# Convolution steps in half-array tiles without swaps, output sums per segment and 128 tokens, and a new written-out order

## The chip, the cores and the metric

The kernel runs on one core of one Trainium2 chip. The metric is device time in microseconds. An execution has five engines with queues of their own: TensorE (PE, with its weight loads PEld), VectorE (DVE), ScalarE (ACT), GpSimd (POOL, nearly unused here) and SP, which issues the transfers. Each works through its own instructions in order and waits on semaphores for the others.

## The reference

Input x has 2048 tokens of 512 features. Two branches are computed from it and mixed with a gate per token.

```
g = sigmoid(sum(x * gate_w))                      # one number per token
# branch a: 32 heads of 16, four segments of 512 tokens
for s in 0..3:
    p  = softmax(q_s k_s^T * 0.25 + causal mask);  dot = p v_s
    mem = phi(q_s) M / (phi(q_s) z + 1e-6)         # M, z: sums over earlier segments
    o_s = sigmoid(beta) * mem + (1 - sigmoid(beta)) * dot
    M += phi(k_s)^T v_s;  z += sum phi(k_s)        # phi(t) = t + 1 if t > 0 else exp(t)
a = concat(o) @ wo
# branch b: a long convolution along the tokens, a kernel of 2048 taps per feature
K[d, l] = Re sum_n C[d,n] exp(dt_d A[d,n] l) dt_d B[d,n]
b = causal_conv(x, K) + x * Dskip                  # the reference takes FFTs of length 4096
out = g * a + (1 - g) * b
```

## The kernel before, in words

**How work gets its order.** build_graph records some 1800 operations with their tiles. A written-out list, ORDER, gives for each operation its place, the engine where there is a choice (evictions from PSUM may go to ScalarE or VectorE) and its buffer; replay and emit put the instructions on the engines in that order and add the semaphores. So nothing is decided at run time: each engine's sequence is that of the list. Matrix multiplies all go through one helper, L687; evictions through L226 (ScalarE) and L227 (VectorE), scaled ones through L229 and L230; transfers through L222 on SP.

**Attention.** For each of four segments and four groups of eight heads (16 pairs), project computes q and k, scores makes five score tiles, so 80 in all. A score tile fills PSUM banks 0 to 3 with multiplies on row tiles of the array (16 or 32 rows, four at a time), is turned into weights by one exponential of 2048 columns (L1069, ScalarE), is masked (L1081, VectorE, or extra multiplies on TensorE for the first eight pairs), and is multiplied with v (pv, 17 columns each). nrm (L1041 to L1044) normalises, mem (L1117 to L1121) adds the memory part, and ophase transposes the result into oT (the operation named oT). All other PSUM users share banks 4 to 7 and, where free, the lower ones.

**Convolution.** ssm_prep, ssm_powers (L795 to L805) and ssm_cb prepare the parameters; x_level1 applies a first level of a 4096-point transform to x over the tokens and stores it in a scratch tensor; tables (L1164, L1167, L1171) builds powers for four groups of 128 features, and lag turns them into kernel taps with multiplies on column tiles of 32 (four at a time). tail then runs, for each half of the 512 features, 16 steps. One step: load two constants (CT of 192 KB, CD of 320 KB) and a piece of the scratch; X, two multiplies of 256 columns, whose real and imaginary parts lie in the two halves of the partitions; an eviction; two transfers of 64 KB that put the halves in swapped places beside it; K, ten multiplies from the taps; an eviction; Y, the product on VectorE (L1273, 1024 columns); V, four multiplies back; an eviction; and a store into V2.

**Output sums.** When tail has a half, it takes its 256 columns for 16 blocks of 128 tokens (every 16th token), two blocks to a PSUM bank: per block four multiplies of attention result with wo (256 columns), two of x with a diagonal matrix (the skip term, 128 columns), two of G2 with V2 (256 columns). Two evictions per bank scale by 1 - g (the branch a was prepared with e^z = g / (1 - g), so one factor serves both), and a store of 256 KB writes four blocks. gate_rows brings the gates into that layout once, with a small multiply. A block holds tokens of all four segments, so no sum can end before the last segment's attention.

**What sets the order there.** In the list all 32 blocks of output sums stand behind the last score and behind the last steps of tail, whose last V steps come between them and the last attention products. Tail's second half starts when the tables' buffers are free, since it lies in their place.

Of the kernel before, what the change touches and what calls it, by code (L numbers as in the profile page):

```python
# [366 lines left out]
9/0 10/1 391/1 15/0 29/0 0/0 23/0/0 24v 30/1 193/0 13/4 14/2 21/0 12/3 11/5 27/1/1 25/2/2 189/0 54/0 31/8 32/0 33/6  # L367
38/2 39/3 57/3 34 190 35 7/0 37/11 20/0 1226/1 28a 36 17/0 45/8 40/4 41 55/4 44/5 26v 46/7 42 173/7 43 48/0 50/9 18/0
51/10 1232/5/0 47 59/1 4/0 56a/0 58v 1244/7/1 1/0 61/4 1242/6 49/12 60 71/0 205/0 62v/0 73/3 178/2 52/0 72 53 85/1
196/3 16/0 74a/3 1234/0 1235a 250/1/0/0 83/0 67/6 1243a 200/4/2/2 65/2 84 191 1233a 208/2 98v/1 181/3 1245a 201a 377/0  # L370
95/1 63 197/0 97/5 86v/9 99 3/0 66 1246 96 192/0 174/0 64 203/5/0 209a 251a 202 107/2 77/1 214/0/0/0 75 76 206/3 1236
108/0 109 252 204a 219/0/3 220 378/2 119/2 79/1 122v/2 110v/4 175/0 198/0 78 379 123 121/4 120 176/0 87 100 588/0 221
253/1/1 240/0/0 241 131/1 177 994v/0 254a 215 179/0 111 133/2 88 998v/0 112 997v 134v/5 1002 1003/0 1247/0 199/1 132
216 210/2 242 145/4 212/1 135 207a 1000/1 146v/6 91/3 1004 228/0/1 229 996v 995v 143/2 89/1 1009/0 144 999 8/0 158v/8
230 147 157/5 213a 255/0/1/1 223/0/2 256 155/2 2/0 799/0 124 1008 1248/3/1 224 90 211a 222/1 1249a 159 1001 1260/2/0
589/3 257 136 225 1250/0 160 1006/1 1010 156 590 1005 1012/0 167v/7 1251a 1252 1014 1258/3 1011 236/0/3 1007 1259a 237
103/0 226 227 231 232/3 1261a 337/0/2 235/3 1013 238 233 168 101/2 800/2 1015/1 1020 234/0 262/0/2 263 239 338a 1262
169 1229/1/1 243 244 801 1016 1263/0/0 102 264 113/1 1230a 1021/0 245/0 217 1227/2 1264a 266/0/1 267 1022 268 1018/1
1265/1 148 1024/0 1023 383/0/1/1 115/7 114 1228a 258 271/0/0 246 127/2 384a 1266a 272 293/2/2/2 273 296/0/0 265/1 1267
279/0/2 280 1231 297a 218/0/0 259 269 270 274 1025 1017 125/2 281 986/0 283/0/3 284 592/0 1032 247 591 1026 1033/0 126  # L380
137/1 1239/3/1 294a 1019 1034 260/0 1237/2 334/0/0/0 285 295 275/1 1035 1240a 307/0/1 308 1268/1 1030/1 278/3 276
1238a 1255/2/0 282 1027/0 335a 277/1 309 1253/1 1289/0 286 287 339/0/0/0 303/0/3 1028 288/1 1254a 1241 1029 340 341
380 304 443/1/1 1036/0 1031 248/0 1037 305 444a 138/4 336 320/0/0 321 289 1256a 1284/1/1 22/0 802 1257 249v/0 1043/2/0
1044 1045 322 290 447/0 139 1046 298/0/1/1 1286/3 1047v 312/0/2 313 194 1285a 182 149/2 150/5 398/2 1287a 195 1038/1
1039 1040 1041 299 301 300 399v 1056v/0 314 1290/3/0 306/0 324/0/3 325 1054v/0 1052v 1291a 1288 1061/1 1053v 1042a
116a/0 310 319/2 1060 1058/0 1055v 311 326 315 1292/3 385 1293a 1048/0 1294 323 1276/1/1 1057 1062 1059 1070/1 316/2
342 1066 1063 346/0/1 347 386/3/0 1277a 317 1069 80v/1 1274/1 318/0 291/0 348 1071 350/0/2 292a 151 351 387a 1300/0/0
1302/3 1067/0 1275a 1078 1079/1 104v/3 1068 1278 327 328 396/1 1080 352 68v/4 81 355/0/0 356 1082/0 1301a 397a 1081
329/3 1073/1 1083 330 1303a 357 349/0 1072 353 1281/1/1 1064/0 331 354 392/3 393a 1282a 1304 1050 1049 1074 1090 69
363/0/3 1091/1 140v/8 1065 364 1075 302/2 358 343 1271/3/0 1092 344 365 359/4 1076/0 1279/1 70 1272a 105 360 141 1280a  # L390
367/0/1 368 369 1051 117 1283 361/1 1085/1 106 1307/2/1 1269/3 1084 1077 1093 1094/0 405/0/2 1086 1270a 1087 406 381
6/0 92a/2 1088/1 407 1095 1089 362/3 1305/1 366 370 1273 1295/0/0 409/0/0 161/1 410 1308a 1306a 411 394/2 490/1/2/2
422/0/3 423 395a 408/2 371 1296a 1297/0 412 413 93 372/1 1309 373 491a 261 440/1/0/0 424 1298a 1310/0 1299 82 94 374
388/0 389 162/0 345 118 1323/1 441a 128v/9 180 163 1390/0 492 426/0/2 427 152v/5 382/0 170v/7 171 442 153 1096/0/1
1097 1098 1099 1101/3 1312/2 332/1 390/1 428 1100a 1102 164a/6 165 333a 414/0/0 415 416 1103 1104 1114v/0 1113v/0 1118
472/0/1 473 417 1119/1 421/0 1325/1 425 448/1/1/1 1110a 1116/0 1105a 1313/3/2 1111a 1120 1112a 474 172 1311/1 429 430
1106 1109 129 130 166 1107 455/0/0 456 1115 1124 1314a 418/5 1128/1 419 1117 420/0 142 1121 431/2 1108 1316 449 450
493/3/0 1324/0 400/2/0/0 457 401 1326/1/0 459/0/3 1327a 460 1125/0 432 1127 433 451 1129 1126 1137/1 1130 1122/0 1136
1317/1/0 1123 461 375/0 1318a 1138 464/0/2 494a 402 465 1315 1338/1 1337/1 466 1139 154 1364/2 1319/1 1328 1329 5/0
541/1/2 458/3 1320/2/0 542a 1321a 476/0/0 462 477 376a 478 1330/1/0 471/2 463 475 1336/0 467 1131/1 1331a 1339/0/2 479  # L400
1340a 520/0/3 480 1140/0 521 403 1141 522 1363/0 1132 1148 1343/1/1 404/0/1 1134/0 1149/1 1344a 452 468/0 1133 481/3
469 1332/0 1342 1341 1322/0 482 495/1 470/1 483 434/1/2/1 512/0/1 1333/1/1 1135 453 435 1334a 1150 1350/1 1351/1 513
514 651/0/0/1 436 1345/1 437 538/1/1/0 1146/0 1346/3/0 1151 1152/1 652a 1347a 524/0/2 498/2/0/0 438/0 1349/1 539a
1352/3/1 439a/0 1362/0 1335 499 803 1353a 1356/1/1 1142 1153 1355 445/0 1354 605/0/0 1365/3/0 1357a 525 519/1 523
1366a 1348 1145 1143/1 1369/3/0 500 1368 597/2/1 526 1144 1367 1370a 606a 598a 1147 1358/0 1389/1 527 528 183/6 529/4
1154/3/0 497/1 446 501 530 1159/0 184/0 1160 1359/2/0 1360a 484/2/1/0 1376/0 546/7/1/1 185/0 1377/1 543/0 540 1371/1
1372/2/1 496 653 547 485 1375/1 486 1416/2 549 487 548 1161 1162 1373a 1388/0 1155 1156 1157 531/0 503/0/2 1374 1163a
187 1378/2/2 1172a/0 1168v/0 504 1169v 1382/1/0 1391/0/1 1170v 1158a 1361 1379a 1174/1 1171v 1177/0 1173 1176 1175
1395/3/1 1429/1 1381 1380 1178 505 1179 1183/1 1182 1428/0 1392a 507/0/0 508 1185 1186/0 1383a 1393 545/0 502/2 1184
1394 1187 609/0 1384/0 550 1442/0 1415/1 1396a 1385/1/0 509 610a 1195/0 553/0/3 1386a 554 506/3 510 1180/1 1194 551  # L410
532/0/5/1 511 515 1414/1 555 1397/1 1398/2/1 1196 516/0 533 517 987/1 518 1399a 1181 557/0/2 599/1 558 534 1417/3/0
1418a 1387 1197 559 1198/0 535 1421/2/0 1427/0 1165 1189/1 1419 1420 1434/3/1 1199 1455/2 1441/1 1188 1430/1/1 1206
1422a 570/0/0 1207/0 571 1431a 594/0/2/2 1167 1433 1432 488/2 1190 1400 1423/0 572 595a 489a 556/1 1208 562/0/1 563
1424/0/0 544 1192/1 1435a 564 654/2/0 655a 1425a 1191 1436/1 1447/3/0 1440/1 574/0/3 1448a 1437/2/1 1193 1210/0 1201/1
603/0 188 1454/0 1443/3/0 1438a 575 604a 1200 560 561 565 1453/0 566/3 1444a 1468/1 536/2 576 1467/1 567 1445 596
1460/0/1 1446 568/1 1456/3/2 616/0/2 1202 1209 1426 537a 1494/0 1457a 569/1 573 577 578 607/2 814/3/1 617 608a 1461a
815a 1204/1 637/0/1 1459 1458 1439 600 1480/0 1449/1 1450/2/0 638 1466/1 1211 1203 1473/3/0 659/0/1/1 1462/0 1474a
1451a 625/0/0 1205 1463/3/1 1217/2/1 1218 1464v 626 1219 1493/1 1469/3/0 1470a 1220 813 620/0/3 1479/0 579/2 618 639
1486/3/1 627 1481/2 602 660 1452 661 619/0 580 1221v 581 621 1212/2 1213 1487v 1471 1472 633/0/2 1403/1 1506/0
1482/1/1 701/3/1/0 988/0 622 623 1483v 704/1/2 624 1507/2 1484 1465 634 454 1475/1 1476/6/0 628 705a 635 593/1 658/1  # L420
1477a 702a 552 629/1 630 1485 1214 1492/1 1215 683/0/3 1499/1/0 632/3 636 1216a 684 703 640 666/0/2 641 1580/0
1495/2/2 631/0 1500a 1582/0 1488/0 1567/1 1489/0/1 1554/2 667 1496v 1512/1/1 670/0/0 1490v 1513a 611/2/0/0 1401/0
1593/3 662 642/4 643 644 582/0/2/1 816/3 668 671 583 1224 584 585 1569/1 1498 1497 731/0/1 1583/0/0 1568/0 612 1478
1402/1 817v 613 749/1/2/2 1570/3/1 732 1404/2/0 1222 1584v 750v 669/0 614 687/0/2 1571a 1405a 1555/1 1595/2 1556/0
601/0 1501/1 1491 672 615/1/0 663 645/1/0/0 664 646 1581/2 757/1/0/0 647 688 648 758 656/1 673 685 674 675/0/0
1502/2/0 1225 759 751 657 1503v 676 586/3 587a 1166 689 1505/1 752/1/1 753a 1164 805/2/0/1 806a 677 695/3/5/1 696 697
# [982 lines left out]
```

## Time and profile before

| what | value |
|---|---|
| three runs | 309.24, 316.8 and 314.4 us; median 314.4 |
| profiled execution, first to last instruction (its span) | 311.0 us; its own time is not given apart |
| mean granted TensorE clock in it | 0.944 of full speed |
| busy: TensorE, VectorE, ScalarE | 264.8, 260.2, 262.7 us |
| instructions: TensorE, VectorE, ScalarE | 4397, 642, 320 |
| exponentials of the scores, L1069 | 80, together 151.9 us |
| moved by the transfers | 45.82 MB, mean 147 GB/s |

How to read the rows: a group of instructions is "line engine operation output<-input shape xcount | busy us, mean ns of one | idle time of the engine just before them, and what ended it". Busy time is the union of the intervals, so for matrix multiplies, which overlap, it is far less than count times mean. PSUM is psum, the on-chip memory is sb. In the table of stretches each engine's number is its busy time in that stretch, with the count of instructions; PEclk is the granted TensorE clock there.

### The profile page before, as it was taken

The page shows a single profiled execution, that of the slowest core. Times are in us where ns is not written, and L with a number is a line of the kernel's source. Part 1 is how long each engine was busy: PE and PEld are TensorE (multiplying, and loading weights), DVE is VectorE, ACT ScalarE, POOL GpSimd, SP SyncE. Part 2 cuts the span into 40 slices and gives each one's busy share as a digit, 9 for nine tenths or more (in the row PEclk, how much of TensorE's full clock was granted, in tenths as well). Part 3 has the DMA queues.
Part 4 walks back from the last instruction along what each step waited for, and adds up shares of the span by engine and source line. Part 5 has one row for each costly group of instructions (what it writes and reads, how often), then busy time and mean ns, then how long its engine had stood idle before and what let it go on. Part 6 is the DMA issues. An engine that isn't in the chain of part 4 may idle for free.

```text
span 311.0 us, 10366 instructions
## 1 busy us (share of the span) xinstructions
PE 264.8 (85%) x4397; PEld 185.1 (60%) x4430; DVE 260.2 (84%) x642; ACT 262.7 (84%) x320; POOL 3.1 (1%) x9
## 2 busy tenths in 40 slices
PE   2678788788779789998999898999999988799991
PEld 1433355454435547676766574676677666579991
DVE  1999899999998889998999868888999898862152
ACT  2999999999999979987999898999999999861150
POOL 2000000000000000000001000000000000000000
PEclk9995689999968779999999999999999999979997
DMA  6878522431232545465555657637555667511143
GB/s 145 280 176 160 142 87 70 124 118 52 83 110 77 160 121 155 147 197 157 158 173 192 199 159 229 196 95 228 156 197 186 200 200 217 168 52 48 38 137 102
DMA packets 54926, 45.82 MB, mean 147 GB/s; under 512 B 22624, under 2 KB 50272, under 8 KB 54880
## 3 DMA queue, kind: packets, MB, share of 16 engines
q1 hardware_dynamic: 54880, 45.16, 49.8%
q8 instruction: 35, 0.57, 0.8%
q14 instruction: 11, 0.09, 0.1%
HBM read 26.92 MB, written 6.29 MB: 107 GB/s over the span
## 4 chain that ended last, share of the span: by engine, by line
ACT 42%; PE 41%; issue 7%; DVE 4%; DMA 3%; SPq 1%; another core or an unknown queue 0%; DVEq 0%; ACTq 0%
PE psum L687 40%; ACT sb L1069 23%; ACT sb L226 13%; ACT sb L795 2%; DMA sb<-sb 1%; DVE sb L227 1%; DMA sb<-c_DNM 1%; DMA sb<-c_ident 1%; SPq L222 1%; ACT sb L803 1%; ACT sb L1000 1%; DVE sb L1273 1%; ACT sb L949 1%; DVE sb L1121 0%; ACT L888 0%
## 5 line engine op out<-in xcount | busy, mean ns | idle before, releaser
L687 PE MATMUL psum<-sb 128*128 128x17 bf16 (+12 forms) x4309 | 257.5, 225 | 32.5 <-ACT sb L1069 14.4
L687 PEld LDWEIGHTS psum<-sb 128*128 128x128 bf16 (+3 forms) x4342 | 178.2, 97 | 109.7 <-issue 29.7
L1069 ACT ACTIVATE sb<-psum 128x2048 bf16<-128x2048 f32 x80 | 151.9, 1899 | 6.7 <-PE psum L687 6.4
L226 ACT ACTIVATE sb<-psum 128x512 bf16<-128x512 f32 (+2 forms) x155 | 88.1, 625 | 8.6 <-PE psum L687 8.1
L227 DVE CAST sb<-psum 128x512 bf16<-128x512 f32 (+1 forms) x47 | 31.3, 676 | 4.8 <-PE psum L687 4.8
L1164 DVE TENSOR_TENSOR sb<-sb 128x512 bf16<-128x512 bf16 (+3 forms) x52 | 33.5, 654 | 0.0
L1167 DVE TENSOR_TENSOR sb<-sb 128x512 bf16<-128x512 bf16 (+3 forms) x52 | 33.3, 650 | 0.0
L1171 DVE TENSOR_TENSOR sb<-sb 128x512 bf16<-128x512 bf16 (+3 forms) x52 | 33.3, 656 | 0.0
L1081 DVE TENSOR_TENSOR sb<-sb 128x1024 bf16<-128x1024 bf16 (+1 forms) x40 | 22.5, 575 | 3.4 <-ACT sb L1069 3.3
L1273 DVE TENSOR_TENSOR sb<-sb 128x1024 bf16<-128x1024 bf16 x32 | 21.6, 678 | 2.6 <-DMA sb<-sb 1.9
L230 DVE TENSOR_SCALAR sb<-psum,sb 128x256 bf16<-128x256 f32 x18 | 8.4, 482 | 16.4 <-PE psum L687 15.2
L229 ACT ACTIVATE sb<-psum,sb 128x256 bf16<-128x256 f32 x14 | 6.2, 472 | 16.8 <-PE psum L687 8.8
L1044 DVE TENSOR_TENSOR sb<-psum,sb 128x256 bf16<-128x256 f32 x32 | 13.3, 418 | 0.3
L795 ACT ACTIVATE sb<-sb 128x512 f32<-128x512 f32 x18 | 11.6, 658 | 0.0
L1041 DVE RECIPROCAL sb<-psum 128x16 f32<-128x16 f32 x32 | 8.0, 251 | 2.3 <-PE psum L687 2.0
L1121 DVE TENSOR_TENSOR sb<-psum,sb 128x512 bf16<-128x512 f32 x12 | 8.2, 686 | 0.2
L743 PE MATMUL psum<-sb 128*128 128x128 bf16 x24 | 3.0, 310 | 6.0 <-DMA sb<-c_ident 5.4
L796 DVE TENSOR_TENSOR sb<-sb 128x256 f32<-128x256 f32 x18 | 7.5, 418 | 0.6 <-ACT sb L795 0.5
L949 ACT ACTIVATE sb<-psum 128x512 bf16<-128x512 bf16 x12 | 7.5, 622 | 0.3 <-PE psum L946 0.3
L1000 ACT ACTIVATE sb<-sb 128x512 bf16<-128x512 bf16 x12 | 7.5, 629 | 0.0
L227 DVE COPY sb<-psum 128x1024 bf16<-128x1024 bf16 x3 | 2.1, 686 | 6.4 <-PE psum L743 6.4
L797 DVE SCALAR_TENSOR_TENSOR sb<-sb 128x256 f32<-128x256 f32 x18 | 7.4, 415 | 0.0
(66 smaller groups left out, 102.0 us busy)
## 6 DMA issues: line engine op xcount, KB each, us to landing
sb<-c_DNM SPq DMA_DIRECT2D x32, 320.0 KB, 3.5
sb<-c_DNM SPq DMA_DIRECT2D x32, 192.0 KB, 3.0
sb<-sb SPq DMA_DIRECT2D x84, 64.0 KB, 2.6
scr_Z<-sb SPq DMA_DIRECT2D x16, 256.0 KB, 2.3
sb<-scr_Z SPq DMA_DIRECT2D x32, 128.0 KB, 3.1
sb<-sb SPq DMA_DIRECT2D x32, 128.0 KB
sb<-in_A_x_dram SPq DMA_DIRECT2D x5, 512.0 KB, 4.6
out_dram<-sb SPq DMA_DIRECT2D x8, 256.0 KB, 2.2
```

Of the source, the lines that this page charges most:

```text
L226: fa = lambda e: e.activation(dst(), src(), ACT.Copy)
L227: fd = lambda e: e.tensor_copy(dst(), src())
L687: mm = lambda e, o_, l, r_, st, sp, **kw: e.matmul(o_, lhsT=l, rhs=r_, start=st, stop=sp, skip_group_check=True, **kw)
L795: op("ACT", ("As", 512), lambda e, sq=sq, Z=Z: e.activation(ap(sq, n=512), ap(Z, n=512), ACT.Square), r=[Z], w=[sq], key=PW[h] + PWS * k)
L949: op("ACT", ("Ax", 512), lambda e: e.activation(ap(ek, n=512), ap(P, n=512), ACT.Exp), r=[P], w=[ek])
L1044: op("DVE", ("V1", 256), lambda e: e.tensor_tensor(ap(o1, gi * 16, [[128, 4], [32, 4], [1, 16]]), ap(T, dims=[[68, 4], [17, 4], [1, 16]]), ...
L1069: o = op("ACT", ("Ax", 2048), lambda e, P=P, pT=pT: e.activation(ap(pT, n=2048), ap(P, n=2048), ACT.Exp, scale=0.25), r=[P], w=[pT])
L1081: op("DVE", ("V2", 128 * nb), lambda e, pT=pT, dims=dims: e.tensor_tensor(ap(pT, dims=dims + [[1, 128]]), ap(pT, dims=dims + [[1, 128]]), ...
L1164: op("DVE", ("V2" if n > 1 else "V1", 256 * n), lambda e: e.tensor_tensor(run(tile, ne, dst, 1), run(tile, ne, src, sstep), ap(pw, cl * 51 ...
L1167: op("DVE", ("V2" if n > 1 else "V1", 256 * n), lambda e: e.tensor_tensor(run(t2, n, 0, 1), run(tile, ne, src, sstep), ap(pw, cl * 512 + 2 ...
L1171: op("DVE", ("V2" if n > 1 else "V1", 256 * n), lambda e: e.tensor_tensor(D_(), D_(), ap(t2, n * 128, [[-n * 128, 2], [2 * n, 64], [1, 2 * ...
L1273: op("DVE", ("V2", 1024), lambda e, Y=Y, XAB=XAB, K3=K3: e.tensor_tensor(ap(Y, dims=[[512, 2], [1, 512]]), ap(XAB, dims=[[512, 2], [1, 512 ...
```

## The change

Tail's steps lose the swap. The two outputs pi of a step now lie in the two halves of the partitions and the real and imaginary parts in columns: X is four multiplies on column tiles of 64, Y reads its operands with repeats instead of a swapped copy, and V is eight multiplies on row tiles of 64, which write two PSUM banks. The two constants become one load of 480 KB. The output sums leave tail: finals(s) makes, for each segment, four groups of 128 tokens with all 512 columns in one bank: 16 skip multiplies and 16 with G2 on four column tiles of 32, then four full multiplies with wo, one eviction of 512 columns and one store of 128 KB. gate_rows goes; gate_tokens computes the gates a second time in the layout of the output with 64 one-column multiplies on column tiles. wo and the output buffers move to the place that tail's first half leaves. ORDER is new throughout; ScalarE gets 319 operations instead of 317, VectorE 625 instead of 642, and SP issues 194 transfers instead of 283. Most groups of finals stand between the scores of the last segment, for the segments 0 to 2 whose attention is then complete.

```diff
@@ gate_tokens
             for tb in range(4):
                 for k in range(4):
                     i = mm(e, ap(P, tb, n=1), ap(xTT[0], k * 2048 + s * 512 + tb * 128, n=128), ap(gwT, k, n=1), k == 0, k == 3)
+            for g4 in range(4):
+                for k in range(4):
+                    for j in range(4):
+                        i = mm(e, ap(P, 4 + g4, n=1, p0=32 * j, np_=32), ap(xTT[0], k * 2048 + s * 512 + 4 * g4 + j, [[16, 32]]), ap(gwT, k, n=1),
+                               k == 0, k == 3, tile_position=(0, 32 * j))
...
@@ tail, one step
-            S.dma(lambda CT=CT: ap(CT, n=768), lambda t=t: hC[t][:, 1280:2048], 196608, w=[CT], key=kx - 6)
-            S.dma(lambda CD=CD: ap(CD, n=1280), lambda t=t: hC[t][:, 0:1280], 327680, w=[CD], key=kx - 6)
+            S.dma(lambda C=C: ap(C, n=1920), lambda t=t: hC[t][:, :], 491520, w=[C], key=kx - 6)
...
-                for pi in range(2):
-                    i = mm(e, ap(PX, pi * 256, n=256), ap(CT, 512 + pi * 128, n=128), ap(Zx, pi * 256, n=256), True, True)
+                for c in range(2):
+                    for pi in range(2):
+                        i = mm(e, ap(PX, c * 256, n=256, p0=64 * pi, np_=64), ap(C, 1664 + pi * 128 + c * 64, n=64), ap(Zx, pi * 256, n=256),
+                               True, True, tile_position=(0, 64 * pi))
...
-            for c in range(2):
-                S.dma(lambda XAB=XAB, c=c: ap(XAB, 512, n=512, p0=64 * c, np_=64),
-                      lambda XAB=XAB, c=c: ap(XAB, 0, n=512, p0=64 - 64 * c, np_=64), 65536, r=[xp[0]], pw=[xp[1 + c], XAB], key=kx)
...
-                ap(Y, dims=[[512, 2], [1, 512]]), ap(XAB, dims=[[512, 2], [1, 512]]), ap(K3, dims=[[0, 2], [1, 512]]), ALU.mult),
+                ap(Y, dims=[[512, 2], [256, 2], [1, 256]]), ap(X, dims=[[256, 2], [0, 2], [1, 256]]),
+                ap(K3, dims=[[0, 2], [256, 2], [1, 256]]), ALU.mult), r=[X, K3], w=[Y])
...
-                for pi in range(2):
-                    for ab in range(2):
-                        i = mm(e, ap(PI, pi * 256, n=256), ap(CT, pi * 256 + ab * 128, n=128), ap(Y, ab * 512 + pi * 256, n=256),
-                               pi == 0 and ab == 0, pi == 1 and ab == 1)
+                for q, blk in enumerate((0, 1, 1, 2)):
+                    for pi in range(2):
+                        i = mm(e, ap(PI, pi * 512, n=256), ap(C, 1280 + blk * 128, n=128, p0=64 * pi, np_=64),
+                               ap(Y, q * 256, n=256, p0=64 * pi, np_=64), q == 0, q == 3, tile_position=(64 * pi, 0))
...
@@ new; the output sums of tail, whose shapes are given above, go
+    def finals(s):
+        for g in range(4):
+            P = S.ps()
+            def f(e, P=P, g=g):
+                for k in range(4):
+                    for j in range(4):
+                        i = mm(e, ap(P, k * 128, n=128, p0=32 * j, np_=32), ap(xTT[0], k * 2048 + s * 512 + 4 * g + j, [[16, 32]]), ap(diagT, k * 128, n=128),
+                               k == 0, False, tile_position=(0, 32 * j))
...
+            def f2(e, P=P, g=g):
+                for h in range(2):
+                    for kt in range(2):
+                        for j in range(4):
+                            i = mm(e, ap(P, h * 256, n=256, p0=32 * j, np_=32), ap(G2T, kt * 128 + 32 * s, n=32),
+                                   ap(V2s[h], ((4 * g + j) * 2 + kt) * 256, n=256), False, False, tile_position=(0, 32 * j))
...
+            for h0, h1 in (((0, 4),) if s < 3 else ((0, 3), (3, 4))):
+                def f3(e, P=P, g=g, h0=h0, h1=h1):
+                    for hg in range(h0, h1):
+                        i = mm(e, ap(P, n=512), ap(oTT[0], hg * 2048 + s * 512 + g * 128, n=128), ap(woT, hg * 512, n=512), False, hg == 3)
...
+            S.evac(lambda ou=ou: ap(ou, n=512), lambda P=P: ap(P, n=512), 512, r=[P, omgP[s]], w=[ou], scale=lambda g=g: ap(omgT, 4 * s + g, n=1))
+            S.dma(lambda g=g: bass.AP(out, (512 * s + 4 * g) * 512, [[512, 4], [8192, 32], [1, 512]]),
+                  lambda ou=ou: ap(ou, n=512), 131072, r=[ou])
```

More of the change, by code (lines that the diff above doesn't have):

```diff
@@ L1124, in ophase @@
         S.tag = "oT%d.%d" % (s, hg)
+        oTp[(s, hg)] = oTT[s].part()
         P3 = S.ps()
@@ L1227, in tail @@
         hC = hCs[0]
-        V2 = Tile(V2aP if half == 0 else V2bP, BF16)
+        V2 = V2s[half]
         hn = "ab"[half]
@@ L1358, in build_graph @@
     tail(1, TK0 + 60.0, TDK)
+    S.key = 260.0
+    for s in range(4):
+        finals(s)
     return S
```

342 lines of the change are left out of this document (146 added, 196 removed).

## The prediction

> **What bounds the kernel now.** I read the page's busy shares, its slices and the shares of the chain that ended last, to see whether one engine holds the whole span.
>
> ```profile
> PE 264.8 (85%) x4397; PEld 185.1 (60%) x4430; DVE 260.2 (84%) x642; ACT 262.7 (84%) x320; POOL 3.1 (1%) x9
> ...
> PE   2678788788779789998999898999999988799991
> ...
> DVE  1999899999998889998999868888999898862152
> ACT  2999999999999979987999898999999999861150
> ...
> ACT 42%; PE 41%; issue 7%; DVE 4%; DMA 3%; SPq 1%; another core or an unknown queue 0%; DVEq 0%; ACTq 0%
> ```
>
> No engine does: three stand within 2% of each other, and the chain passes between ScalarE and TensorE. Only the last five slices (about 39 us) differ: TensorE stays at 9, the two others fall away. The scores pace the program: each of the 80 steps ends in an exponential, L1069. So I cut the span at the ends of the 5th, the 30th and the last of them, read off ScalarE's instructions in time (the last one below), and at the end of the last scaled eviction, and took the busy time of each stretch.
>
> ```profile
> 272.66 1.88 ACT L1069 ACTIVATE sb<-psum 128x2048 bf16<-128x2048 f32 x1
> ```
>
> ```profile
> core 0: us, PE busy (x) PEld busy (x) DVE busy (x) ACT busy (x) POOL busy (x), PEclk, DMA share, GB/s
> 0.00:41.30 41.30, 27.17 (x235) 14.64 (x240) 33.02 (x107) 34.30 (x53) 1.88 (x7) 0.83 0.71 177
> 41.30:121.40 80.10, 65.84 (x1370) 40.77 (x1381) 75.49 (x185) 76.79 (x97) 0.00 (x0) 0.91 0.35 103
> 121.40:274.50 153.10, 141.93 (x2477) 102.99 (x2489) 138.75 (x324) 142.75 (x155) 1.22 (x2) 0.99 0.59 180
> 274.50:305.50 31.00, 29.82 (x329) 26.71 (x326) 12.94 (x28) 8.84 (x20) 0.00 (x0) 0.97 0.26 78
> 305.50:311.00 5.50, 0.00 (x0) 0.00 (x0) 0.00 (x1) 0.00 (x0) 0.00 (x0) 0.64 0.21 61
> ```
>
> Stage 2 (exponentials 6 to 30) is ScalarE's and VectorE's (76.8 and 75.5 of 80.1). In stage 3 (31 to 80) all three lie between 138.8 and 142.8 of 153.1, so whichever gets more work has about 11 us to spare. Stage 4 is TensorE alone, which the chain of waits confirms:
>
> ```profile
> 274.42 4.45 PE psum L687 x69
> 278.88 0.14 issue
> 279.02 25.46 PE psum L687 x260
> 304.48 0.02 issue
> 304.50 0.50 DVE sb L230
> ```
>
> Those 30 us are the output sums, and no score is left to run beside them. After them come 5.5 us for the last stores and SP's closing waits, which the change leaves as they are.
>
> **The change part by part.** The prices, from the groups kept apart by shape (busy total, then the mean of one), and from TensorE's instructions in time:
>
> ```profile
> L687 PE MATMUL psum<-sb 128*32 128x20 bf16 x1024 | 10.5, 176 | 2.8 <-issue 2.5 <-DVE sb L1171 0.2
> L687 PEld LDWEIGHTS psum<-sb 128*32 128x32 bf16 x1024 | 9.0, 93 | 5.3 <-issue 3.8 <-ACT sb L226 0.8 <-DVE sb L1171 0.5
> L687 PE MATMUL psum<-sb 16*128 16x512 bf16 x64 | 6.5, 398 | 4.1 <-ACT sb L1069 2.3 <-ACT sb L226 1.6
> L226 ACT ACTIVATE sb<-psum 128x512 bf16<-128x512 f32 x147 | 83.7, 627 | 8.4 <-PE psum L687 7.9 <-remote 0.3
> L227 DVE CAST sb<-psum 128x512 bf16<-128x512 f32 x45 | 30.4, 685 | 4.8 <-PE psum L687 4.8
> L1273 DVE TENSOR_TENSOR sb<-sb 128x1024 bf16<-128x1024 bf16 x32 | 21.6, 678 | 2.6 <-DMA sb<-sb 1.9 <-ACT sb L226 0.6
> L230 DVE TENSOR_SCALAR sb<-psum,sb 128x256 bf16<-128x256 f32 x18 | 8.4, 482 | 16.4 <-PE psum L687 15.2 <-ACT sb L229 0.9
> L229 ACT ACTIVATE sb<-psum,sb 128x256 bf16<-128x256 f32 x14 | 6.2, 472 | 16.8 <-PE psum L687 8.8 <-DVE sb L230 7.8
> ```
>
> ```profile
> 170.85 0.49 PE L687 MATMUL psum<-sb 128*128 128x256 bf16 x3
> ```
>
> ```profile
> 171.07 0.27 PE L687 MATMUL psum<-sb 128*128 128x256 bf16 x1
> 171.18 0.38 PE L946 MATMUL psum<-sb 128*128 128x128 bf16 x4
> 171.54 0.29 PE L687 MATMUL psum<-sb 16*128 16x256 bf16 x4
> ```
>
> ```profile
> 195.35 0.40 PE L946 MATMUL psum<-sb 128*128 128x128 bf16 x4
> 195.59 0.17 PE L687 MATMUL psum<-sb 128*128 128x17 bf16 x1
> ```
>
> *Tiles beside each other.* The change cuts TensorE's array: X in two column tiles of 64, the inverse V in two row tiles of 64, the skip term, the convolution's last sum and the gate rows in four column tiles of 32. The before has both kinds: 64 score multiplies of 512 columns on row tiles are busy 6.5 us, 0.10 each although one lasts 0.40, so four run together; 1024 on column tiles of 32 take 10.5 us, 0.010 each. The shapes with 64 are not in the trace. The price lies between nothing (side by side) and one after another: V 128, X 64 and the last sums 192 multiplies of 256 columns more, at 0.11 us (three take 0.49, one 0.27), and the skip term 192 of 128 columns at half of that, 53 us together. I take 0, where both rows stand. Then TensorE streams as many columns as before in every step (16 groups x 3584 columns in the output sums, 32 x 1792 before), and only the gate rows are new: 256 one-column multiplies x 0.010 = 2.6 us.
>
> The Trainium skill, "TensorEngine Tiling (Array Packing)", Restrictions, says that column tiling switches Fast Weight Load off. With the load time of "TensorE: Matmul & The Clock Gate", LDWEIGHTS (columns / 1.2 ns), this gives an estimate of 27 ns for each 32-column load, and of some 8 us in all if the loads came one after another, so 321 in place of the sum below. The row of 1024 such loads, busy 9.0 us, speaks against that: 9 ns each.
>
> *Changing the shape of the tiles.* Four transposes of 128 columns followed by a full-array multiply: next start after 0.24 us (195.35 to 195.59). Four followed by a row-tiled multiply: 0.36 (171.18 to 171.54). So a change of shape costs about 0.1 us. Counted in the two orders, TensorE changes shape 176 times before and 302 times after: 10, 58, 108, 0 by stage against 14, 64, 208, 16. That adds 12 us to TensorE, 10 of them in stage 3. Hidden where TensorE would have waited anyway (0), at most 0.12 each; I take 0.1.
>
> *Swaps gone.* 64 transfers of 64 KB go, and L1273's waits for them: 1.9 us in all. In stage 3 VectorE has 14 us to spare, so I count 0. One load of 480 KB per step replaces two, and SP issues 194 transfers instead of 283; DMA has 3% of the chain, so again 0 (at most those 9 us). L1273 keeps its size and its unbroken runs of 256, so 678 ns stays (nothing less; double, 22 us, if its mode were lost: not taken).
>
> *Output sums moved into the scores.* Each group now needs one segment's attention and both halves of V. In the new order the last V stands some ten scores before the end, and of 16 groups 9 are finished on TensorE ahead of the last exponential; stage 4 keeps 7. They sit between scores on TensorE's queue, so a sum that waits for the last store of V, or for the output weights, holds the scores behind it. V's last step stands behind the 73rd exponential and the first sum behind the 75th, the load of the weights some six exponentials ahead; two exponentials are 3.8 us, so both are covered. Without cover they would cost about what transfers of their sizes take to land, 3.1 and 4.6 us:
>
> ```profile
> sb<-scr_Z SPq DMA_DIRECT2D x32, 128.0 KB, 3.1
> ...
> sb<-in_A_x_dram SPq DMA_DIRECT2D x5, 512.0 KB, 4.6
> ```
>
> Scaled evictions become 16 of 512 columns (0.63 or 0.69) for 32 of 256 (0.47 or 0.48): 4 us less, over two engines.
>
> *New order.* Work that stands ahead of each mark, by kind times its duration:
>
> - Stage 1: ScalarE gets 2.4 us more (squares and copies of the powers): +2.
> - Stage 2: VectorE gets 9.1 us more (10 more table steps, three level-one evictions), ScalarE 0.7: VectorE would need 75.5 + 9.1 = 84.6 of 80.1. Nothing if it may run late, since scores don't wait for tables; 9 if it also keeps its 4.6 of idle; I take +4.
> - Stage 3: ScalarE +4.2 (8 evictions), VectorE -7. TensorE gets 36 multiplies of 512 columns (twice 0.11 each, 7.8), 9 last sums (four rounds of 256 columns each, 3.9), 11 skip terms (four of 128, 2.5) and 2 us of V and K from stage 4, gives 4 us to stage 2, and pays 10 for shapes: +22. 141.9 + 22 = 164 of 153.1. Were it without any idle, +11; with today's 11 us of idle, +22; if shapes and sums hid behind ScalarE, +4. Stage 4 before, where TensorE alone sets the pace, has it busy 29.8 of 31.0, so I take +13, near the lower end.
> - Stage 4: 28 multiplies of 512 columns (6.0), 7 last sums (3.1), 5 skip terms (1.1), the last attention products (2.5) and 16 changes of shape: 14.4 us from the last score, of which the exponential covers 1.9, plus 1 of waits and 0.6 of eviction: 14 for 31, so -17.
>
> **The sum** against the profiled span: 311 + 2 + 4 + 13 - 17 = 313. The page gives no time for this execution but its span, which lies inside the runs shown (309.2 to 316.8, median 314.4, 1.1% above it). I keep 313 as the time: the ends of each term are wider than that gap.
>
> **The rivals.** One row of the list of waits goes ahead (total, times, longest):
>
> ```profile
> PE psum L687 <- ACT sb L1069: 14.4, 28, 1.7
> ```
>
> 1. *ScalarE sets stage 3.* Scores pace the kernel, shapes and sums fall into TensorE's waits. For it: ScalarE has 42% of the chain. Against: 22 us don't fit into 11 of idle. Stage 3 +4, stages 1 and 2 +2: 311 + 4 + 2 - 17 = 300.
> 2. *TensorE keeps its idle time (slower).* The scores hold four PSUM banks, and each output sum holds one of the other four from its skip term to its eviction; TensorE, in order, waits for banks as often as now. Stage 3 +22, stage 2 +4, stage 1 +2: 322. It decides for slower once stage 3 passes about 170 us. For it: TensorE's longest releasers are ScalarE's rows (14.4 us at L1069). Against: with TensorE last, ScalarE will have evicted before it is asked.
> 3. *The tiles run one after another.* Then the change doesn't do what it says, and TensorE gets the 53 us: 366. Against: both rows of tiles above.
>
> **How the numbers follow.** Forecast 0.43 (its own range 306 to 318), rival 1 0.30, rival 2 0.24, rival 3 0.03. From 299 to 324 leaves out the lower part of rival 1 and rival 3. About 2% (6 us) is what a measurement of this kernel can tell from no change. Rival 1 is faster than that, rivals 2 and 3 slower, the forecast within: 0.30, 0.43, 0.27.
>
> **What would show it.** Right: stage 4 at some 14 us; stage 3 at 160 to 170 with TensorE above 95% busy and ScalarE below 92%; a gap of 0.1 us at each change of shape around X, V and the sums; groups of four column tiles of 256 columns starting 0.11 to 0.12 apart. Wrong: TensorE under 92% in stage 3 with ScalarE above 93% (rival 1); TensorE waiting 20 us and more for evictions (rival 2); 256-column tiles starting one after another (rival 3).

## The result, and the profile after

The changed kernel takes 325.9 us (median of 4 runs, 325.8 to 327.9) where the kernel before takes 314.5 (309.2 to 316.8). Executions more than 1.5% above the fastest of their kernel are left out of the ratios and, further down, of the medians (of the profiles used only that of dense_stores is such a one), so the ratio is 1.049, 95% interval 1.042 to 1.056, where these medians give 1.036. To the 313.4 us that the kernel before takes in most of the later rounds it would be 1.040. It is slower, by more than the range of the forecast (299 to 324) allowed for.

I cut the profiled execution as before: at the ends of the 5th, 30th and 80th exponential and of the last scaled eviction. The table of stretches of the changed kernel:

```profile
core 0: us, PE busy (x) PEld busy (x) DVE busy (x) ACT busy (x) POOL busy (x), PEclk, DMA share, GB/s
0.00:45.38 45.38, 30.18 (x428) 18.03 (x433) 36.91 (x111) 36.46 (x58) 1.87 (x7) 0.92 0.66 165
45.38:124.99 79.61, 65.42 (x1432) 42.42 (x1447) 78.11 (x186) 77.25 (x96) 0.64 (x1) 0.98 0.32 94
124.99:300.38 175.39, 165.06 (x3052) 110.40 (x3072) 141.84 (x319) 148.83 (x164) 0.66 (x1) 0.99 0.45 138
300.38:314.05 13.67, 12.56 (x257) 7.76 (x252) 3.78 (x12) 5.57 (x9) 0.00 (x0) 1.00 0.20 64
314.05:324.13 10.08, 0.00 (x0) 0.00 (x0) 0.00 (x0) 0.00 (x0) 0.00 (x0) 0.71 0.17 58
```

Beside the rows of before: stage 1 +4.1, stage 2 -0.5, stage 3 +22.3, stage 4 -17.3, the end +4.5; +13.1 in all. Stage 4 fell as forecast. Stage 3 grew by what TensorE got more to do there, 23.1 us (165.06 for 141.93), and its idle time nearly stayed, 10.3 for 11.2. The shares of the chain that ended last, on the page of the changed kernel, say the same: TensorE has 56% of it, ScalarE 31%, where the two had 41% and 42%.

```profile
PE 273.2 (84%) x5154; PEld 178.6 (55%) x5196; DVE 260.6 (80%) x625; ACT 268.1 (83%) x322; POOL 3.2 (1%) x9
...
PE 56%; ACT 31%; issue 4%; DVE 3%; DMA 2%; SPq 1%; ACTq 0%; DVEq 0%
```

The growth lies in the last 30 scores. Of each kernel I took the stretch from the 50th to the 80th exponential, where the granted clock is 0.99 and 1.00 in these two. First before, then after:

```profile
195.70:274.50 78.80, 73.56 (x1134) 53.65 (x1139) 70.87 (x171) 75.73 (x72) 0.00 (x0) 0.99 0.59 179
```

```profile
202.00:300.40 98.40, 94.99 (x1608) 62.50 (x1621) 75.12 (x170) 82.23 (x82) 0.00 (x0) 1.00 0.45 136
```

Before, ScalarE is busy 75.7 of 78.8 us and paces; after, TensorE is busy 95.0 of 98.4. TensorE got 21.4 us more into a stretch with 5.2 us of its idle time, and 19.6 came out as time.

Cut further, into fives of exponentials, the growth is uneven (us, in brackets TensorE's busy time): 66 to 70 took 12.5 (11.7) before and take 19.3 (18.9) after, 76 to 80 took 11.9 (10.0) and take 20.3 (19.6). These ten scores hold 15 of the 19.6 us. The new list packs steps of tail into the first of these fives (five of their products Y, for one before), where ScalarE too is busy 16.6 us for 11.7, and output sums into the second.

### The profile page after: what moved, and what is told of

Read it like the earlier page. It is cut to its first block, busy times and chain, and to the rows that moved or that the text cites. A ratio compares the mean times of both kernels' runs of the same rounds, so it can differ in the third digit from the quotient of the medians.

```text
span 324.1 us, 11751 instructions
## 1 busy us (share of the span) xinstructions
PE 273.2 (84%) x5154; PEld 178.6 (55%) x5196; DVE 260.6 (80%) x625; ACT 268.1 (83%) x322; POOL 3.2 (1%) x9
## 4 chain that ended last, share of the span: by engine, by line
PE 56%; ACT 31%; issue 4%; DVE 3%; DMA 2%; SPq 1%; ACTq 0%; DVEq 0%
PE psum L673 56%; ACT sb L1045 17%; ACT sb L226 8%; ACT sb L781 2%; DMA sb<-in_B_log_dt_dram 2%; ACT sb L924 1%; ACT sb L789 1%; DVE sb L227 1%; SPq L222 1%; DVE sb L1246 0%; PE psum L921 0%; ACT L879 0%; DVE sb L752 0%; DVE sb L748 0%; ACT sb L229 0%
## 5 line engine op out<-in xcount | busy, mean ns | idle before, releaser
L673 PE MATMUL psum<-sb 128*128 128x17 bf16 (+12 forms) x5066 | 266.9, 227 | 35.4 <-ACT sb L1045 13.5
L673 PEld LDWEIGHTS psum<-sb 128*128 128x128 bf16 (+4 forms) x5108 | 172.0, 102 | 128.0 <-issue 40.6
L1045 ACT ACTIVATE sb<-psum 128x2048 bf16<-128x2048 f32 x80 | 150.8, 1885 | 16.6 <-PE psum L673 15.7
L226 ACT ACTIVATE sb<-psum 128x512 bf16<-128x512 f32 (+1 forms) x150 | 85.0, 606 | 14.8 <-PE psum L673 14.4
L227 DVE CAST sb<-psum 128x512 bf16<-128x512 f32 (+1 forms) x52 | 35.1, 683 | 7.4 <-PE psum L673 6.8
L1141 DVE TENSOR_TENSOR sb<-sb 128x512 bf16<-128x512 bf16 (+3 forms) x52 | 34.3, 667 | 0.1
L1144 DVE TENSOR_TENSOR sb<-sb 128x512 bf16<-128x512 bf16 (+3 forms) x52 | 34.3, 664 | 0.1
L1148 DVE TENSOR_TENSOR sb<-sb 128x512 bf16<-128x512 bf16 (+3 forms) x52 | 34.0, 668 | 0.2
L229 ACT ACTIVATE sb<-psum,sb 128x512 bf16<-128x512 f32 x12 | 7.8, 685 | 4.6 <-PE psum L673 4.6
L1093 DVE SCALAR_TENSOR_TENSOR sb<-psum,sb 128x32 f32<-128x32 f32 x12 | 2.3, 189 | 9.3 <-PE psum L673 9.0
L789 ACT ACTIVATE sb<-sb 128x512 bf16<-128x512 f32 x10 | 6.4, 654 | 0.0
L230 DVE TENSOR_SCALAR sb<-psum,sb 128x512 bf16<-128x512 f32 x4 | 2.9, 749 | 4.2 <-PE psum L673 4.1
```

Of the source, the lines that this page charges most:

```text
L226: fa = lambda e: e.activation(dst(), src(), ACT.Copy)
L227: fd = lambda e: e.tensor_copy(dst(), src())
L673: mm = lambda e, o_, l, r_, st, sp, **kw: e.matmul(o_, lhsT=l, rhs=r_, start=st, stop=sp, skip_group_check=True, **kw)
L1045: o = op("ACT", ("Ax", 2048), lambda e, P=P, pT=pT: e.activation(ap(pT, n=2048), ap(P, n=2048), ACT.Exp, scale=0.25), r=[P], w=[pT])
L1141: op("DVE", ("V2" if n > 1 else "V1", 256 * n), lambda e: e.tensor_tensor(run(tile, ne, dst, 1), run(tile, ne, src, sstep), ap(pw, cl * 51 ...
L1144: op("DVE", ("V2" if n > 1 else "V1", 256 * n), lambda e: e.tensor_tensor(run(t2, n, 0, 1), run(tile, ne, src, sstep), ap(pw, cl * 512 + 2 ...
```

## The experiments

Medians and ratios to the kernel before with 95% interval, and from the profiles the stage 3, the stretch of the exponentials 51 to 80 in it, stage 4 and the end (us). For steps_only and steps_only_full only the ratio and the median are used. The ratio of after was taken to a lower time of the kernel before than the others, so whole times are compared by their medians.

| kernel | median | ratio | stage 3 | 51 to 80 | stage 4 | end |
|---|---|---|---|---|---|---|
| before | 312 to 314 | 1 | 153.1 | 78.8 | 31.0 | 5.5 |
| before_few_waits | 309.8 | 0.990 [0.986, 0.994] | 154.8 | 79.5 | 30.2 | 2.7 |
| before_tiled | 318.0 | 1.017 [1.007, 1.026] | 158.9 | 81.8 | 33.0 | 5.5 |
| before_two_banks | 343.6 | 1.098 [1.089, 1.107] | 182.2 | 92.2 | 31.5 | 5.6 |
| steps_only | 346.8 | 1.108 [1.103, 1.114] | | | | |
| steps_only_full | 338.0 | 1.080 [1.072, 1.087] | | | | |
| after | 325.9 | 1.049 [1.042, 1.056] | 175.4 | 98.4 | 13.7 | 10.1 |
| few_waits | 324.6 | 1.037 [1.031, 1.043] | 172.4 | 98.4 | 13.7 | 7.3 |
| steps_full | 325.8 | 1.039 [1.031, 1.047] | 171.0 | 95.5 | 13.7 | 10.1 |
| sums_full | 330.1 | 1.056 [1.046, 1.065] | 173.7 | 96.0 | 11.8 | 10.4 |
| all_full | 321.5 | 1.027 [1.021, 1.032] | 164.4 | 93.0 | 11.8 | 10.4 |
| sums_last | 335.5 | 1.071 [1.064, 1.078] | 169.2 | 92.7 | 32.6 | 6.7 |
| dense_stores | 320.5 | 1.024 [1.011, 1.037] | 175.8 | 98.4 | 13.7 | 5.0 |
| xl_later | 325.6 | 1.040 [1.027, 1.054] | 172.4 | 98.4 | 13.7 | 10.1 |
| steps_one_bank | 325.7 | 1.040 [1.036, 1.045] | 176.9 | 95.5 | 13.7 | 10.1 |

Stage 3 as a whole moves by some 3 us between executions in which it has one and the same instruction stream: 175.4 and 175.8 in after and dense_stores, where TensorE halts for 3.8 and 3.5 us in all inside the taps' multiplies (last section), 172.4 in few_waits and xl_later, where it halts for 1.3 and 0.8. The exponentials 51 to 80 repeat within 0.1 us (98.4 in all four), so that column carries the verdicts on stage 3.

### Does each change of tile shape cost time?

Theory A: TensorE paces stage 3 and the shapes add to its path. Theory B: they fall into waits that the order makes. Three kernels give back full-array multiplies over the same columns.

```diff
@@ steps_full: X
-                for c in range(2):
-                    for pi in range(2):
-                        i = mm(e, ap(PX, c * 256, n=256, p0=64 * pi, np_=64), ap(C, 1664 + pi * 128 + c * 64, n=64), ap(Zx, pi * 256, n=256),
-                               True, True, tile_position=(0, 64 * pi))
+                for pi in range(2):
+                    i = mm(e, ap(PX, pi * 256, n=256), ap(C, 1664 + pi * 128, n=128), ap(Zx, pi * 256, n=256), True, True)
@@ sums_full: the convolution's last sum (skip term and gates likewise)
-                        for j in range(4):
-                            i = mm(e, ap(P, h * 256, n=256, p0=32 * j, np_=32), ap(G2T, kt * 128 + 32 * s, n=32),
-                                   ap(V2s[h], ((4 * g + j) * 2 + kt) * 256, n=256), False, False, tile_position=(0, 32 * j))
+                        i = mm(e, ap(P, h * 256, n=256), ap(G2T, kt * 128, n=128), ap(V2s[h], (4 * g * 2 + kt) * 256, n=256), False, False)
```

> The changed kernel with X as two and V as four full multiplies of 256 columns (the right columns are streamed, the products are others, so the output is not the reference's). It keeps every column that TensorE streams and takes away 81 of its 302 changes of tile shape, 78 of them in stage 3. Theory A (TensorE paces stage 3 and each change adds 0.1 us to its path): stage 3 goes from 175.4 to about 167.5, the time from 326 to about 318. Theory B (what the order makes TensorE wait for sets stage 3, the changes fall into those waits): stage 3 stays within 2 us, the time at 324 to 327, and TensorE idles about 8 us more.

> The changed kernel with the skip term, the convolution's last sum and the gate rows as full multiplies of the same columns (the products are others, so the output is not the reference's). 41 changes of tile shape go: 4 in stage 1, some 20 in stages 2 and 3, 15 in stage 4; the second set of gate multiplies falls from 256 to 64. Theory A: -4 us for the changes and up to -4 for the gates, so 318 to 322, with 1.5 us of it in stage 4. Theory B: only stage 4 gains, 324 to 325.

> Both edits together (other products, so the output is not the reference's): 302 changes of tile shape become 180, 99 of the 122 in stage 3, about as many as the kernel before has (176). Theory A: stage 3 at about 165, the time 312 to 315. Theory B: stage 3 at 173 to 176, the time 322 to 325.

The list of waits shows what the changes are to TensorE: time before a weight load in which nothing is waited for ("issue"; total, times, longest). Over the whole span that row holds the halts too (40.6 us in after, 37.0 in xl_later, with the same 302 changes), so here it is for the exponentials 51 to 80, where none falls. Before, after, steps_full, sums_full and all_full:

```profile
PEld psum L687 <- issue: 3.7, 17, 0.2
```

```profile
PEld psum L673 <- issue: 15.1, 62, 0.4
```

```profile
PEld psum L673 <- issue: 9.6, 38, 0.4
```

```profile
PEld psum L673 <- issue: 11.3, 49, 0.4
```

```profile
PEld psum L673 <- issue: 5.6, 24, 0.4
```

Counted in the traces, the stretch holds 60, 125, 83, 102 and 60 changes, so against after each is 0.13 to 0.18 us of this row. In the time the stretch falls from 98.4 to 93.0 in all_full, 0.08 for each of 65 changes, to 95.5 in steps_full (0.07 for each of 42) and to 96.0 in sums_full (0.10 for each of 23).

```profile
204.80:297.80 93.00, 90.54 (x1232) 63.25 (x1232) 74.57 (x170) 81.87 (x83) 0.00 (x0) 1.00 0.47 143
```

So theory A holds in kind: stage 3 of all_full is 8 us under that of few_waits, 164.4 for 172.4 (A said 165, B 173 to 176). In the whole time only 4.4 of the 11 to 14 us arrived, and for steps_full none. In the profiles the stage 2 of both is longer than after's (87.3 and 84.0 for 79.6), at a clock of 0.92 and 0.90 for 0.98; few_waits, with after's stream, took 83.6 there at 0.88, so the edits need not be the cause. sums_full came out 4 us slower than the changed kernel, against both theories: its stage 4 gained 1.8 us (1.5 expected), its stage 2 took 89.7 us at a clock of 0.85 with two halts of TensorE of 2 us. Why they fall there is not settled.

The same question asked of the kernel before, with no product changed:

```diff
@@ before_tiled: X (V likewise)
-                    i = mm(e, ap(PX, pi * 256, n=256), ap(CT, 512 + pi * 128, n=128), ap(Zx, pi * 256, n=256), True, True)
+                    for c in range(2):
+                        i = mm(e, ap(PX, pi * 256, n=256, p0=64 * c, np_=64), ap(CT, 512 + pi * 128 + c * 64, n=64), ap(Zx, pi * 256, n=256),
+                               True, True, tile_position=(0, 64 * c))
```

> The kernel before with X and V on column tiles of 64: twice as many multiplies of 256 columns, two at a time, the same products in the same places; order, banks, swaps and sums untouched, the result whole. 263 changes of tile shape for 176, 78 of the added 87 in stage 3. Theory A (TensorE paces stage 3): stage 3 from 153 to 160 or 161, the time 319 to 322. Theory B (its idle time takes the changes): stage 3 within 2 us, the time 312 to 316.

4.7 us in the median (2 to 8 by the interval), between A (6 to 9) and B (up to 3).

```profile
120.32:279.24 158.92, 149.61 (x2647) 101.65 (x2660) 140.66 (x326) 144.53 (x154) 1.20 (x2) 0.99 0.59 174
```

TensorE's busy time in stage 3 grows by 7.7 us (149.61 for 141.93), 0.1 for each of the 78 changes, the stage by 5.8. In the exponentials 51 to 80, where ScalarE sets the pace, 44 changes add 4.5 us to TensorE's busy time and 3.0 to the time. So some two thirds of each 0.1 us reach the time even there.

### Did moving the sums between the scores pay?

The edit is in the written-out list alone: the entries of the sums leave their places, as here, and follow the last exponential (976).

```diff
-932/0/2 933 1684/3 926 921 918/0 905/1 1679/2 906v
+932/0/2 933 926 921 918/0 905/1 906v
```

> The changed kernel with all 16 groups of output sums, their evictions and stores behind the last score; nothing else moves, the result is whole. Some 14.5 us of TensorE's work goes from stage 3 to stage 4. Theory A (TensorE paces both, so the move bought nothing): stage 3 from 172 to 175 down to 158 to 161, stage 4 up to 28 to 30, the time within 4 us of 326. Theory B (the sums filled TensorE's waits between scores, so the move did pay): stage 3 falls by 5 us at most, the time is 333 to 338.

The time rises by 10 us, as theory B said. Stage 3 gives back only 6, stage 4 takes 19 and the end gives 3.4. The exponentials 66 to 70 take 19.3 us here too, so what they gained is not the sums' doing. Without the sums the last five scores of sums_last look like this (stretch 266.4 to 279.0: the five before):

```profile
266.40:279.00 12.60, 9.73 (x198) 6.60 (x194) 10.69 (x25) 11.88 (x12) 0.00 (x0) 1.00 0.45 117
279.00:294.30 15.30, 7.90 (x152) 4.88 (x154) 5.42 (x14) 9.92 (x7) 0.00 (x0) 0.55 0.00 1
```

No engine is full. The chain of that stretch shows ScalarE and TensorE taking turns over the one set of four banks:

```profile
284.62 1.89 ACT sb L1045
286.51 0.05 issue
286.55 0.64 PE psum L673 x4
287.20 0.02 issue
287.22 1.89 ACT sb L1045
289.10 0.05 issue
289.15 0.64 PE psum L673 x8
289.81 1.89 ACT sb L1045
```

A score can't begin before the exponential of the one before it has read the banks: 2.6 us for each of the last three, 1.9 of it the exponential, in which this chain leaves TensorE free. But the granted clock is 0.55 here. In before the same turn of TensorE, at full clock, takes 0.43 us in place of 0.64, and a score 2.4:

```profile
269.83 0.43 PE psum L687 x8
```

So a part of the 10 us is the clock's. An estimate: TensorE has 35% of the chain of these 15.3 us, 5.4 us, and at full clock would need some 3.0 for it, so 2 to 3 us. The sums fill the waits between the scores: the 14.5 us of them (94.99 busy for 80.48 in the exponentials 51 to 80) cost 5.7 there, some 8 with the clock allowed for.

### The steps alone, and the second bank of V

steps_only gives the kernel before the lines of tail's X, Y and V from the change, with the constant of the new layout; steps_only_full takes its X and V back to full multiplies as steps_full does.

```diff
@@ steps_only, V
-            PI = S.ps()
+            PI = S.ps(2)
...
-                for pi in range(2):
-                    for ab in range(2):
-                        i = mm(e, ap(PI, pi * 256, n=256), ap(CT, pi * 256 + ab * 128, n=128), ap(Y, ab * 512 + pi * 256, n=256),
+                for q, blk in enumerate((0, 1, 1, 2)):
+                    for pi in range(2):
+                        i = mm(e, ap(PI, pi * 512, n=256), ap(CT, blk * 128, n=128, p0=64 * pi, np_=64),
+                               ap(Y, q * 256, n=256, p0=64 * pi, np_=64), q == 0, q == 3, tile_position=(64 * pi, 0))
```

> The kernel before with the new steps alone: no swaps, X on column tiles of 64, V on row tiles of 64 into two banks; the output sums, the gate rows, the two constants per step and the order stay (V moves by a place where no pair of banks is free). The result is whole. 264 changes of tile shape for 176, 76 of the added 88 in stage 3. Theory A (TensorE paces stage 3, 0.1 us a change): stage 3 about 7.5 us longer, the time 317 to 321 for 313. Theory B (changes fall into waits that the order makes anyway): 310 to 314, the swap's 1.9 us of waits gained.

> The same with X as two and V as four full multiplies of the same columns (other products, so the output is not the reference's): 176 changes of shape, as before; still no swaps and two banks for V. Theory A: 311 to 314, 6 to 8 us under the new steps alone. Theory B: within 2 us of the new steps alone. If the second bank of V costs by itself, both stand above 315.

Both theories missed, 347 and 338 us. The pair differ by 9 us, near the 6 to 8 of theory A, but both stand 25 to 33 above before, as the last sentence of the second expectation had it for a second bank that costs by itself. The two share that PSUM bank for V and a list bent to it, so the kernel before got only these:

```diff
@@ before_two_banks
-            PI = S.ps()
+            PI = S.ps(2)
```

> The kernel before with two PSUM banks held for each V, one of them unused; banks and some places of the list are given anew as for the new steps alone, nothing else changes, the result is whole. If the bank (and the list bent to it) made the 28 to 34 us of the new steps alone: 335 to 342, stage 3 at 180 to 185. If the steps themselves did: 312 to 318.

```profile
120.75:302.97 182.22, 149.85 (x2477) 104.63 (x2488) 140.58 (x324) 145.00 (x156) 1.20 (x2) 0.95 0.50 151
```

343.6 us: the bank, with the list bent to it, makes the loss, and TensorE sits idle 32 of 182 us. Which of the two it is, the bank or the hundred entries of the list that moved or changed their bank with it, was not separated. Whether it also costs the changed kernel, whose list was written with it:

```diff
@@ steps_one_bank, from steps_full
-            PI = S.ps(2)
+            PI = S.ps(banks=[(b,) for b in (4, 6, 0, 2)])
```

> The changed kernel with X and V as full multiplies, as in steps_full, and V in the first of its two banks alone (other products, so the output is not the reference's); order and places are those of the changed kernel, only the waits that the second bank makes are gone. If the second bank is what still makes TensorE wait 6 to 10 us in stage 3: stage 3 falls from 171 to 164 to 167 and the time to 319 to 322. If the order that was made for two banks has room for them: stage 3 within 2 us of 171, the time 324 to 327.

The exponentials 51 to 80 take 95.5 us, as in steps_full: there the second bank is free. (Its stage 3 as a whole holds two halts of TensorE, 3.6 and 1.8 us.) So the idle time that TensorE keeps in the changed kernel isn't made by it.

### The end

> The changed kernel; SP's closing list waits only for the 16 stores of the output, in place of a wait for each of 120 semaphores. Nothing else changes and the result is whole. Theory C (the list itself holds up the end, with four gaps of 1.3 us): the stretch after the last eviction goes from 10.05 us to 4 to 6, the time from 326 to 320 to 322. Rival: the end waits for the landing of the last store or for what lies behind the program, and the time stays within 1 us.

```diff
@@ few_waits, before_few_waits
+                    used = {id(d) for o in self.order for d in o.waits}
                     for k in range(len(dsem)):
-                        if dcnt[k]:
+                        if dcnt[k] and id(duse[k]) not in used:
```

The end fell by 2.8 us, to 7.3, and the four gaps stayed: theory C held only for a part.

> The kernel before, SP's closing list waiting for the output's stores alone; the result is whole. The changed kernel gained 2.8 us of end by the same edit. If its list cost more because of gaps of 1.3 us that the kernel before doesn't have, here 1 to 2 us go and the end falls from 5.5 to 4; if each wait costs as much in both, 2.5 to 3.5 us go.

Here it fell by 2.9, to 2.7. So each wait of the list costs about the same in both (46 in the changed kernel, 0.06 us apart), and the 4.5 us by which the ends differ are something else. SP's waits in the changed kernel, with the semaphores of the last five stores (172 to 176) told from the rest:

```
store issued    311.47  312.06  312.64  313.23  314.07
its semaphore      172     173     174     175     176
wait passed     315.61  316.90  318.15  319.54  320.89
```

The gaps are landings, 1.3 us apart, the last one 6.8 us after its issue. A store of before, 256 KB, lands 2.2 us after its issue:

```profile
out_dram<-sb SPq DMA_DIRECT2D x8, 256.0 KB, 2.2
```

```diff
@@ dense_stores
-            S.dma(lambda g=g: bass.AP(out, (512 * s + 4 * g) * 512, [[512, 4], [8192, 32], [1, 512]]),
+            S.dma(lambda g=g: bass.AP(out, (512 * s + 128 * g) * 512, [[512, 128], [1, 512]]),
```

> The changed kernel; each output store writes its 128 rows of 1 KB one behind another instead of as 4 runs of 32 rows with a stride (so the rows stand in another order than the reference's). Theory K (a store whose outer count is 4 runs on four of the 16 DMA engines, 1.36 us each, and the five last ones queue): the last store lands 1.5 to 2.5 us after the last eviction instead of 6.8, the end is 5.5 to 6.5 us for 10.05, the time 321 to 323. Rival (the landings are late for what they write to, not for their shape): the end stays within 1 us of 10.

```profile
317.84:322.86 5.02, 0.00 (x0) 0.00 (x0) 0.00 (x0) 0.00 (x1) 0.00 (x0) 0.79 0.15 54
```

```profile
out_dram<-sb SPq DMA_DIRECT2D x16, 128.0 KB, 1.7
```

The end falls by 5.0 us, to 5.0, the median by 5.4, and a store lands after 1.7: theory K. In the trace, the five last stores of the changed kernel bring 20 packets of 4 bytes, 4 each, those of dense_stores and of before 16 each. The Trainium skill, "DMA: Bandwidth & Descriptors", section "Why a DMA increments its semaphore by 16 and not by 1", has the rule: a transfer issued by SP runs on the largest number of engines, up to 16, that divides the slowest dimension of both its patterns, and each of them writes the semaphore once. The slowest dimension of the store is 4 in the changed kernel and 128 in the two others; the trace agrees.

### The start

```diff
-11/2 6/0 1231/1/0 19/0 10/3 16/0 12/4 189 190 193 56/2 54/3 1/0
+11/2 6/0 19/0 10/3 16/0 12/4 189 190 193 56/2 54/3 1231/1/0 1/0
```

> The changed kernel with the first level-one multiply, which waits 7 us for its constant, put behind the two first transposes on TensorE; nothing else moves, the result is whole. Theory D (that wait holds back the first scores): the first exponential starts 2 us earlier (26.5 to 27 for 28.7), the time 323 to 325. Rival (what else stands ahead of the first score decides): start and time within 1 us.

The first exponential starts at the same 28.72 us: the rival. What holds it is ScalarE's list. After the table is loaded, before goes straight to it, the changed kernel does seven other things first. ScalarE's instructions in time (start, length), before and after:

```profile
23.11 1.28 ACT L888 ACT_TABLE_LOAD   x1
24.40 0.21 ACT L888 ACTIVATE sb<-sb 128x4 f32<-128x4 f32 x1
24.51 1.86 ACT L1069 ACTIVATE sb<-psum 128x2048 bf16<-128x2048 f32 x1
```

```profile
23.85 1.28 ACT L879 ACT_TABLE_LOAD   x1
...
25.26 0.58 ACT L924 ACTIVATE sb<-psum 128x512 bf16<-128x512 bf16 x1
25.73 0.62 ACT L781 ACTIVATE sb<-sb 128x512 f32<-128x512 f32 x1
26.25 0.59 ACT L924 ACTIVATE sb<-psum 128x512 bf16<-128x512 bf16 x1
26.73 0.60 ACT L226 ACTIVATE sb<-psum 128x512 bf16<-128x512 f32 x1
27.21 1.16 ACT L789 ACTIVATE sb<-sb 128x512 bf16<-128x512 f32 x2
28.25 0.61 ACT L226 ACTIVATE sb<-psum 128x512 bf16<-128x512 f32 x1
28.72 1.89 ACT L1045 ACTIVATE sb<-psum 128x2048 bf16<-128x2048 f32 x1
```

0.7 us later at the table and 3.5 behind it, 4.2 for the stage's 4.1. This is read off the trace; a list that puts the exponential first was not tried.

**A version that beats both** is before_few_waits: 309.8 us, 1.0% under the kernel before (0.986 to 0.994).

## Why the prediction was wrong, point by point

The sum said 313, and the span is 324.1: stage 3 is 9.3 us of the difference, the end 4.5, stage 1 2.1, stage 4 -0.3 and stage 2 -4.5.

- *Stage 4, 14 us.* Right: 13.67, TensorE busy 12.56 of it.
- *Tiles lie beside each other.* Right. The groups of the changed kernel, by shape:

```profile
L673 PE MATMUL psum<-sb 64*128 64x256 bf16 x256 | 19.4, 278 | 1.4 <-ACT sb L1045 0.9 <-DVE sb L1246 0.5
...
L673 PE MATMUL psum<-sb 128*64 128x256 bf16 x128 | 12.3, 283 | 0.0
...
L673 PE MATMUL psum<-sb 128*32 128x256 bf16 x256 | 9.7, 274 | 0.0
...
L673 PE MATMUL psum<-sb 128*32 128x1 bf16 x256 | 4.6, 201 | 0.0
```

  A multiply of 256 columns alone lasts 0.27 us; on four column tiles 256 of them are busy 9.7, 0.04 each, and the rounds of four start 0.11 us apart. Rival 3 is out. The gate rows took 4.6 us for 2.6. The loads of 32 columns are 13 ns each (1792 of them, busy 23.8 us), not the 27 of the prediction's estimate; how its 8 us came from 27 ns for 768 new loads, which would be 21 us, is not shown there.
- *302 changes at 0.1 us.* Right in size: 0.1 of TensorE's busy time in before_tiled, and 0.07 to 0.10 in the time of the last 30 scores.
- *Stage 3, +13.* **This is the step that failed.** TensorE's work was forecast well, 164 us for 165; what I took off it, nearly all of the 11 us of idle time, mostly did not go away. It is 10.3 us in the changed kernel, 6.0 and 8.2 in the profiles of few_waits and xl_later, whose stage 3 is the same stream; one to four us of each are halts. I had reasoned from stage 4 before, where TensorE alone is 96% busy, but the idle time and the new work lay in different places: in the first 20 scores of stage 3, which held 6 of the 11 us, TensorE's work grew by only 1.7 us (time 77.0 us, 74.0 in few_waits, for 74.3), and in the last 30, where 21 us of work went, there were 5 us to fill. Within these 30, the ten scores 66 to 70 and 76 to 80 alone grew by 15 us. The bound of +22, which I had written beside it, is what came.
- *Stage 2, +4.* It came as -0.5, at a granted clock of 0.98 for 0.91. The same stream at 0.88, in few_waits, took 83.6, 3.5 over before: the size was about right at a like clock.

```profile
45.00:128.56 83.56, 71.98 (x1446) 44.71 (x1447) 78.01 (x187) 77.66 (x96) 0.65 (x1) 0.88 0.30 90
```

- *Stage 1, +2.* The engine was right (ScalarE), the size not: I counted what ScalarE gets more in the stage, 2.4 us, and not what stands ahead of its first exponential, 4.2.
- *The end, "which the change leaves as they are".* Wrong, +4.5: the store's new pattern runs on 4 engines, and the five last stores queue. The pattern stood in the diff.
- *Rivals.* Rival 1 is out: ScalarE is busy 85% of stage 3. Rival 2's time, 322, and its stage 3, +22, came nearest, and "TensorE keeps its idle time" is mostly right; its mechanism, waits for banks, is not shown: the second bank costs nothing in this order, and TensorE's waits for exponentials before a load fell in stage 3, from 7.7 to 6.7 us. ScalarE's waits for TensorE rose instead, from 4.0 to 14.3. Stage 3 in before and after:

```profile
PEld psum L687 <- ACT sb L1069: 7.7, 22, 0.7
...
ACT sb L1069 <- PE psum L687: 4.0, 7, 1.5
```

```profile
ACT sb L1045 <- PE psum L673: 14.3, 27, 2.3
...
PEld psum L673 <- ACT sb L1045: 6.7, 15, 1.4
```

The gain on stage 4 was real, and sums_last shows it net: 10 us, 7 to 8 with the clock allowed for. It was eaten by the shapes (some 8 us in stage 3 by all_full), the start (4), the end (4.5) and the work of TensorE that no wait covered. Of the 19.6 us in the last 30 scores, all_full takes back 5.4 and sums_last 5.7; the rest, 8 to 9 us, no experiment assigns. The steps that the new list packs into the scores 66 to 70, where 6.8 us came about, are the likely place; a list that spreads them was not tried.

## What to carry to other kernels

Work moved under another engine's pace is free only up to the idle time of the very stretch that it lands in: cut that stretch finely (here the last 30 scores, 5 us idle, and in them single fives of scores) before taking any of it off. Where a diff rewrites a transfer's pattern, read its slowest dimension, and look at what lands last. Price a second buffer in the order that has to hold it: the same bank, with the list bent to it, came with 30 us in one kernel and with nothing measurable in another, whose list was written with it.

## What was unexpected on the chip

- A store of 128 KB whose slowest dimension is 4 lands every 1.3 us, so five of them end 6.8 us after the last issue; the same bytes in a pattern of 128 land in 1.7.
- TensorE halts for 0.8 to 3.8 us, up to four times in an execution, with nothing to wait for in the trace, mostly among the taps' multiplies on column tiles of 32: 4.4 us in all in before, 3.8 after, 4.9 in steps_full, 5.8 in sums_full, 0.8 in xl_later. The granted clock often falls soon behind a long one: in the changed kernel a halt ends at 180.6 us, and the clock is 0.50 from 181.8 to 185.2. The cause is open.
- Stage 2 of one and the same stream took 79.6 us at a granted clock of 0.98 and 83.6 at 0.88.
